# Heads 2 to 30 of an attention kernel: values stationary in the array by quadrants, row sums and normalising on VectorE, the exponent's bound from weight lengths

## The chip, the cores and the metric

The kernel runs on one core of a Trainium2 chip. The metric is the device time of one execution in microseconds (us). A change of less than 0.2% of it is about what a measurement of this kernel cannot tell from none. The engines are named as the profile names them: PE is TensorE's matmuls and PEld its weight loads, DVE is VectorE, ACT is ScalarE, POOL is GpSimd, SP is SyncE, which here only issues DMAs.

## The reference

```
xn = layernorm(x)                                    # x: 2048 x 640, bf16
q  = (xn @ wq)  -> 32 heads of 2048 x 192
s  = softmax(q k^T / sqrt(192)) v                    # k, v: 32 x 2048 x 192
b  = (silu(xn @ w1) * (xn @ w3)) @ w2                # hidden width 1536
out = x + (s @ wo) * silu(b)                         # wo: 6144 x 640
```

## The kernel before

**Tiling.** A head is worked on in four quarters (`qb`) of 512 queries. A quarter has eight steps (`p`), each of which takes 256 keys: two key tiles of 128. Scores come out transposed, keys on the partitions and queries along the row, in a PSUM tile `st2` of 128x1024, of which there are two, used in turn. ScalarE takes the exponent of a whole tile at once into `pT2` (bf16), so no transposition is needed ahead of the values.

**Scores** (`scores`, L472). A head has 192 channels, three times 64. Each matmul contracts 64 channels, so that two of them, one on the upper and one on the lower 64 rows of the array, work at a time. A step has three such pairs, each streaming 512 queries. `qS` and `qD` (made by POOL, L367 and L371) and `KM` (L136, L139) are copies of the queries and keys with their halves swapped, so that every operand stands on the right rows.

**Values** (`values`, L519). The probabilities are the stationary operand, 64 keys by 128 queries, and the values stream: 192 channels and a column of ones, which yields the row sums. That is 193 columns, eight pairs of matmuls a step. The upper and the lower row half accumulate into two parts of each of the two PSUM tiles `ob0` and `ob1`.

**End of a quarter** (`evict`, L493). For each of the two PSUM tiles DVE copies one part (L500), adds the other (L501), takes the reciprocal of the row sums (L506) and scales into the staging tile `ostage` (L507). Every second head, four staging tiles are stored to `o_scr` by DMA (L511).

**The projection of the next head** (`project_chunk`, L340) runs inside the current one: at step 1 of each quarter, `extra` puts ten pairs of 512-column matmuls for one quarter of head h+1 (and, in the spare columns, of the gated layer's hidden units) into a tile of the same two-slot PSUM pool as the scores. DVE casts both halves to `qA` and `qF` (L363, L364).

**The bound of the exponent** (`finish_head`, L447). Softmax is taken without a running maximum. A bound of the scores is subtracted instead: for each channel the largest |k| (six DVE reductions a head, L386) times the largest |q| (two reductions a quarter, L375), summed over channels.

**What sets the order.** Instructions wrapped in `pin` keep the order in which the program issues them on their engine. `advance` (L545) issues scores and the exponent of a step and keeps a list `parts` of pending value matmuls, of which three or four are left when the next step starts; this is why PE always has work while ScalarE computes. Loads of the keys and values of head h+2 are issued on SP at the start of head h (L116, L119), weights on POOL's queue (L105). Head 0 has a hand-written order; heads 1 to 31 run through the loop at L745. After the last head come the rest of the gated layer and the output projection (L820 on), which the diff leaves as they are.

Of the kernel before, what the change touches and what calls it, by code (L numbers as in the profile page):

```python
# [16 lines left out]
P = 128  # L17
# [13 lines left out]
def _kernel_impl(ctx, tc, A_x, A_k_cache, A_v_cache, A_wq, A_wo, B_w1, B_w3, B_w2, out):  # L31
# [124 lines left out]
    with ExitStack() as actx:  # L156
        qp = actx.enter_context(tc.tile_pool(name="qp", bufs=2))
        pp = actx.enter_context(tc.tile_pool(name="pp", bufs=4))
# [150 lines left out]
        def start_head(h):  # L309
            L = loads.pop(h)  # L310
            heads[h] = dict(
                h=h, L=L,
                qA=qp.tile([P, SQ], BF16, tag="qA", name="qA"),
                qF=qfp.tile([P, SQ], BF16, tag="qF", name="qF"),
                qS=qp.tile([P, SQ], BF16, tag="qS", name="qS"),
                qD=qp.tile([DT, SQ], BF16, tag="qD", name="qD"),
                st=stt.tile([P, 5, NQB], F32, tag="st", name="st"),
            )
            pin(nc.vector.memset(heads[h]["st"][:], 0.0))
# [20 lines left out]
        def project_chunk(h, qb, cast=nc.vector.tensor_copy, mid=()):  # L340
# [6 lines left out]
            if h == 0 and qb > 0:  # L347
                by_halves(halves, lambda t, c: wq[:, t, c, :], qs, nc.scalar.copy if qb == 1 else nc.vector.tensor_copy, steps((parts.pop(0),), *mid))
            elif h == 0:
                acc["bp"] = ps_o.tile([P, 2, 512], F32, tag="ob0", name="bp")  # L350
                halves[1] = acc["bp"][:, 1, :]
                for u in (slice(0, 256), slice(256, 512)):
                    for t in range(2):
                        for c in range(DC):
                            pin(nc.tensor.matmul(halves[t][:, u], lhsT=wq[:, t, c, :], rhs=xnT[:, c, u],
                                                 start=(c == 0), stop=(c == DC - 1)))
            else:
                for s in range(2 * DC):
                    for t in range(2):
                        xs = xnT if s % 2 == t else xnS  # L360
                        pin(nc.tensor.matmul(halves[t], lhsT=wq[ROWS[t], s, :], rhs=xs[ROWS[t], s // 2, qs],  # L361
                                             start=(s == 0), stop=(s == 2 * DC - 1)))
            pin(cast(out=qA[:, qs], in_=halves[0]))  # L363
            pin(cast(out=qF[:, qs], in_=halves[1]))  # L364
# [12 lines left out]
            return maxima  # L377
# [6 lines left out]
        def key_maxima(h, j, k=0, n=1):  # L384
            c0, c1 = k * HALF // n, (k + 1) * HALF // n
            pin(nc.vector.tensor_reduce(out=heads[h]["st"][:, j, k:k + 1], in_=heads[h]["L"]["KT"][:, j, c0:c1], axis=AX.X,  # L386
                                        op=ALU.max, apply_absolute_value=True))

# [83 lines left out]
        def scores(hd, qb, p, fill=(0, 0, 0), st2=None):  # L472
# [8 lines left out]
            for s, step in enumerate(steps):  # L481
                keep_busy(fill[s])
                for t, (k, q) in enumerate(step):
                    pin(nc.tensor.matmul(st2[:, t * 512:(t + 1) * 512], lhsT=k, rhs=q[ROWS[t], qs],  # L484
                                         start=(s == 0), stop=(s == 2)))
            return st2

        def weights(st2, nb):
            pT2 = pp.tile([P, 1024], BF16, tag="pT2", name="pT2")
            pin(nc.scalar.activation(out=pT2[:], in_=st2[:], func=ACT.Exp, scale=SCALE, bias=nb[:]))  # L490
            return pT2

        def evict(hd, qb, b, ob):  # L493
            h, hg = hd["h"], hd["h"] % HG
            if b == 0 and hg == 0:
                acc[qb] = stp.tile([P, 4, HG * DH], BF16, tag=f"ostage{qb}", name="ostage")
            ostage = acc[qb]
# [5 lines left out]
            def rest():  # L503
# [3 lines left out]
                pin(nc.vector.tensor_tensor(out=ostage[:, b * 2:b * 2 + 2, hg * DH:(hg + 1) * DH], in0=osum[:, :, 0:DH],  # L507
                                            in1=rl.unsqueeze(2).to_broadcast([P, 2, DH]), op=ALU.mult))
                if b == 1 and hg == HG - 1:
                    g0 = h - hg  # L510
                    acc["store"] = nc.sync.dma_start(  # L511
                        out=o_scr[qb].rearrange("(t p) c -> p t c", p=P)[:, :, g0 * DH:(g0 + HG) * DH], in_=ostage[:, :, :])
# [6 lines left out]
        def values(hd, qb, p, pT2, by_bank=False):  # L519
# [17 lines left out]
            if p == NPAIR - 1 or by_bank:  # L537
                return [lambda b=b: part((0, 1), (b,)) for b in range(2)]
            return [lambda t=t: part((t,), (0, 1)) for t in range(2)]
# [5 lines left out]
        def advance(hd, qb, p, extra=None):  # L545
            pT2 = weights(scores(hd, qb, p), hd["nb"][qb])
            parts.extend(values(hd, qb, p, pT2))
            while len(parts) > (4 if extra else 3):
                parts.pop(0)()
            if extra:  # L550
                extra()
            while late:
                late.pop(0)()

# [47 lines left out]
        def lead():  # L602
            hd, nb = heads[0], heads[0]["nb"][0]
            vals = [values(hd, 0, p, weights(st2, nb), p < 2) for p, st2 in enumerate(early)]
# [4 lines left out]
            vals.append(values(hd, 0, 3, weights(scores(hd, 0, 3), nb)))  # L609
# [3 lines left out]
            vals.append(values(hd, 0, 4, weights(st2, nb)))  # L613
# [9 lines left out]
            parts.extend(vals[4])  # L623
# [4 lines left out]
        def next_part():  # L628
            parts.pop(0)()
# [51 lines left out]
        hTp = fstack.enter_context(tc.tile_pool(name="hTp", bufs=2, side="right"))  # L681
# [8 lines left out]
        def get_hT(qb):  # L690
            if qb not in hTs:
                hTs[qb] = hTp.tile([P, FC - 1, 512], BF16, tag="hT", name="hT")
# [29 lines left out]
        def hidden_last(qb):  # L722
# [3 lines left out]
            for s in range(2 * DC):  # L726
                for t in range(2):
                    xs = xnT if s % 2 == t else xnS
                    pin(nc.tensor.matmul(ps[:, t * 512:(t + 1) * 512], lhsT=w[ROWS[t], s, :], rhs=xs[ROWS[t], s // 2, qs],  # L729
                                         start=(s == 0), stop=(s == 2 * DC - 1)))  # L730
# [14 lines left out]
        for h in range(1, H):  # L745
# [13 lines left out]
            key_slots = list(all_keys)  # L759
            chunks = [[0], [1], [2], [3]] if h + 1 < H else [[0, 1], [2, 3], [], []]  # L760
            gated = []
            for qb in range(NQB):
                post = []

                def extra():
                    if h % 2 == 1:
                        for c in chunks[qb]:
                            gated.append(swiglu_chunk(h // 2, heads[h - 1]["qF"], hd["qF"], c))
                    if h + 1 < H:
                        post.append(project_chunk(h + 1, qb))  # L770
                    else:
                        post.append(hidden_last(qb))

                for p in range(NPAIR):
                    advance(hd, qb, p, extra if p == 1 else None)
# [5 lines left out]
                    if p > 4 and gated:  # L781
                        gated.pop(0)()
                    if h + 1 < H:
                        if p == 2:
                            post.pop()()
                            if qb == NQB - 1:
                                finish_head(h + 1)
                        elif p > 3 and key_slots and (h > 1 or qb > 0):
                            next_keys(h + 1, key_slots)
                    elif p == 3:  # L790
                        gated.append(post.pop()())
            heads.pop(h - 1, None)

# [16 lines left out]
        while len(parts) > 3:  # L810
            parts.pop(0)()
        rest = ffn_hidden(0, 1, ps_st.tile([P, 1024], F32, tag="st2", name="ps_gu"), parts.pop(0))
        load_hT(1)
        while parts:
            parts.pop(0)()
# [331 lines left out]
```

## Time and profile before

| | |
|---|---|
| median of 3 runs | 1937.28 us (1936.53 to 1937.6) |
| the profiled execution: first to last instruction | 1935.5 us |
| granted TensorE clock | 1.000 |
| PE busy | 1927.5 us, 100% of the span |
| ACT busy | 1213.5 us, 63% |
| DVE busy | 1091.5 us, 56% |
| POOL busy | 457.9 us, 24% |
| HBM read and written | 54.26 MB, 31.98 MB |

Rows of the profile's groups name the line, the engine, the operation, what is written and read, the shape and the count, then the busy time, the mean ns of one and the idle time of the engine ahead of them. The timeline lists single instructions with their start and length. A matmul's length in it includes its way through the array, so two rows of the same pair length overlap; the pace is read from the starts.

### The profile page before, as it was taken

How to read it: one execution, taken by the hardware profiler on the slowest of the kernel's cores; microseconds unless marked ns; L12 is line 12 of the kernel's file. 1: busy time of each engine (PE TensorE's matmuls, PEld its weight loads, DVE VectorE, ACT ScalarE, POOL GpSimd, SP SyncE). 2: the span in 40 equal slices, each digit the busy share in tenths (PEclk: the TensorE clock that was granted, in tenths of full speed). 3: DMA queues.
4: the chain of work that ended last, by engine and by line, in shares of the span. 5: the costliest groups of instructions: out<-in, count | busy, mean ns of one | idle time of the engine just before them, and what ended most of it. 6: DMA issues, size and time to landing. Idle time of an engine off the chain costs nothing.

```text
span 1935.5 us, 59521 instructions
## 1 busy us (share of the span) xinstructions
PE 1927.5 (100%) x26720; PEld 1266.1 (65%) x26743; DVE 1091.5 (56%) x2240; ACT 1213.5 (63%) x1173; POOL 457.9 (24%) x757
## 2 busy tenths in 40 slices
PE   9999999999999999999999999999999999999999
PEld 5666666666666666666666677666666666454446
DVE  8665656565656565666655666656665655521111
ACT  7777777777767677777777777777777777210000
POOL 3432222222222222233222222222222220000000
PEclk9999999999999999999999999999999999999999
DMA  7621313121212222242223222213131102946763
GB/s 172 133 71 41 80 41 79 42 71 38 59 41 65 52 55 62 57 95 68 63 50 71 50 71 49 71 41 79 42 79 38 43 10 90 262 93 144 166 151 77
DMA packets 340355, 148.31 MB, mean 77 GB/s; under 512 B 291632, under 2 KB 333584, under 8 KB 340096
## 3 DMA queue, kind: packets, MB, share of 16 engines
q1 hardware_dynamic: 327152, 114.84, 25.7%
q0 software_dynamic: 8256, 24.58, 4.8%
q10 hardware_dynamic: 4688, 5.05, 0.8%
q8 instruction: 210, 3.44, 0.8%
q14 instruction: 49, 0.40, 0.1%
HBM read 54.26 MB, written 31.98 MB: 45 GB/s over the span
## 4 chain that ended last, share of the span: by engine, by line
PE 99%; ACT 0%; issue 0%; DVE 0%; POOL 0%
PE obank L530 35%; PE st L484 34%; PE ps L361 14%; PE ps_s L891 8%; PE ps_s L847 3%; PE ps_f L911 2%; PE ps_gu L704 1%; PE ps_f L927 1%; PE ps L729 0%; PE ps L330 0%; PE fill L207 0%; PE pst L272 0%; PE ps_gu L330 0%; ACT xnT L273 0%; POOL qS L367 0%
## 5 line engine op out<-in xcount | busy, mean ns | idle before, releaser
L490 ACT ACTIVATE pT<-st,nb 128x1024 bf16<-128x1024 f32 x1016 | 1130.8, 1113 | 435.1 <-PE st L484 434.7
L530 PEld LDWEIGHTS <-pT 64*128 64x128 bf16 x16384 | 713.8, 94 | 242.0 <-ACT pT L490 1.5
L530 PE MATMUL obank<-vt,pT 64*128 64x193 bf16 x16384 | 852.3, 243 | 0.2 <-ACT pT L490 0.2
L500 DVE COPY osum<-obank 128x386 f32<-128x386 f32 x256 | 142.4, 556 | 551.4 <-PE obank L530 551.4
L484 PE MATMUL st<-qS,KM 64*128 64x512 bf16 x1023 | 385.2, 377 | 0.5 <-POOL qS L367 0.5
L484 PE MATMUL st<-qD,KT 64*128 64x512 bf16 x1023 | 385.2, 377 | 0.0
L484 PE MATMUL st<-qS,KT 64*128 64x512 bf16 x1023 | 385.1, 376 | 0.1
L484 PE MATMUL st<-qA,KT 64*128 64x512 bf16 x1023 | 385.2, 377 | 0.0
L484 PE MATMUL st<-qA,KM 64*128 64x512 bf16 x1023 | 385.2, 376 | 0.0
L484 PE MATMUL st<-qF,KT 64*128 64x512 bf16 x1023 | 385.1, 376 | 0.0
L367 POOL COPY qS<-qA 64x512 bf16<-64x512 bf16 x256 | 189.4, 740 | 513.8 <-DVE qA L363 482.3
L484 PEld LDWEIGHTS <-KT 64*128 64x128 bf16 x4096 | 202.2, 94 | 135.8 <-issue 0.6
L361 PE MATMUL ps<-xnT,wq 64*128 64x512 bf16 x1240 | 288.1, 376 | 0.0
L361 PE MATMUL ps<-xnS,wq 64*128 64x512 bf16 x1240 | 287.0, 377 | 0.0
L361 PEld LDWEIGHTS <-wq 64*128 64x128 bf16 x2480 | 120.6, 94 | 116.2
L507 DVE TENSOR_TENSOR ostage<-osum,rl_all 128x384 bf16<-128x384 f32 x256 | 153.4, 599 | 8.8
L891 PE MATMUL ps_s<-oT,wo_sb 128*128 128x512 bf16 x705 | 154.9, 379 | 0.8
L501 DVE TENSOR_TENSOR osum<-osum,obank 128x386 f32<-128x386 f32 x256 | 142.6, 557 | 8.9
L891 PEld LDWEIGHTS <-wo_sb 128*128 128x128 bf16 x720 | 70.4, 98 | 85.0 <-issue 0.2
L386 DVE TENSOR_REDUCE st<-KT 128x1 f32<-128x512 bf16 (+1 forms) x189 | 122.0, 685 | 1.2
L484 PEld LDWEIGHTS <-KM 64*128 64x128 bf16 x2048 | 101.0, 94 | 16.5 <-issue 0.5
L105 POOL DMA_DIRECT2D wq<-in_A_wq_dram x62 | 45.7, 737 | 272.8 <-PE ps L361 260.4
(136 smaller groups left out, 1174.6 us busy)
## 6 DMA issues: line engine op xcount, KB each, us to landing
o_scr<-ostage SPq DMA_DIRECT2D x64, 384.0 KB, 2.8
vt<-in_A_v_cache_dram SPq DMA_DIRECT2D x62, 384.0 KB, 4.9
wo_sb<-in_A_wo_dram POOLq DMA_DIRECT2D x1, 7680.0 KB, 32.6
wq<-in_A_wq_dram POOLq DMA_DIRECT2D x31, 160.0 KB, 3.3
hT_scr<-hblk SPq DMA_DIRECT2D x16, 256.0 KB, 3.0
xnS<-xnT POOLq DMA_DIRECT2D x8, 320.0 KB, 7.0
wq<-in_B_w_dram POOLq DMA_DIRECT2D x31, 80.0 KB, 2.6
wq<-in_A_wq_dram POOLq DMA_DIRECT2D x31, 80.0 KB, 2.9
```

The source lines that it names most:

```text
L105: keep(nc.gpsimd.dma_start(out=wq[ROWS[t], :, c0:c1], in_=w.rearrange("(s p) d -> p s d", p=DT)))
L361: pin(nc.tensor.matmul(halves[t], lhsT=wq[ROWS[t], s, :], rhs=xs[ROWS[t], s // 2, qs], start=(s == 0), stop=(s == 2 * DC - 1)))
L367: keep(nc.gpsimd.tensor_copy(out=qS[ROWS[t], qs], in_=qA[ROWS[1 - t], qs]))
L386: pin(nc.vector.tensor_reduce(out=heads[h]["st"][:, j, k:k + 1], in_=heads[h]["L"]["KT"][:, j, c0:c1], axis=AX.X, op=ALU.max, apply_absolu ...
L484: pin(nc.tensor.matmul(st2[:, t * 512:(t + 1) * 512], lhsT=k, rhs=q[ROWS[t], qs], start=(s == 0), stop=(s == 2)))
L490: pin(nc.scalar.activation(out=pT2[:], in_=st2[:], func=ACT.Exp, scale=SCALE, bias=nb[:]))
L500: pin(nc.vector.tensor_copy(out=osum[:], in_=ov[:, 0, :, 0:DH + 1]))
L501: pin(nc.vector.tensor_tensor(out=osum[:], in0=osum[:], in1=ov[:, 1, :, 0:DH + 1], op=ALU.add))
L507: pin(nc.vector.tensor_tensor(out=ostage[:, b * 2:b * 2 + 2, hg * DH:(hg + 1) * DH], in0=osum[:, :, 0:DH], in1=rl.unsqueeze(2).to_broadcas ...
L530: pin(nc.tensor.matmul(acc["o"][b][:, r, (j % 2) * 256:(j % 2) * 256 + DH + 1], lhsT=pT2[ROWS[r], t * 512 + j * P:t * 512 + (j + 1) * P], ...
L847: pin(nc.tensor.matmul(ps, lhsT=oT[:, k, :], rhs=wo_sb[:, k, c0:c1], start=(k == 0), stop=(k == OC - 1)))
L891: pin(nc.tensor.matmul(ps_of[d], lhsT=wo_sb[:, k, d * P:(d + 1) * P], rhs=part(k // KQ)[:, k % KQ, :], start=(k == 0), stop=(k == OC - 1)))
```

## The change

It concerns heads 2 to 30 (`in_quads`).

- **Values** (`values_quads`): the values are now stationary, in blocks of 64 keys by 64 channels, and the probabilities stream. A step streams, for each of the two key tiles, the first 128 channels ("high": four matmuls, one per quadrant of the array, of 512 queries) and the last 64 channels ("low": the two column halves of the array take the two halves of the queries, four matmuls of 256). The output is transposed, channels on the partitions. The column of ones is not used.
- **Scores and projection** in these heads are issued by quadrants too: each matmul with 128 weight columns becomes two with 64.
- **Row sums** (`row_sums`): DVE adds the probability tiles in bf16, two steps' tile at a time: two additions of 2048 a quarter (`fours`), one `join` of 2048, one `fold` of 1024, one of 512 (`ends`). A DMA transpose of the 128x512 result brings the queries onto the partitions; `turned_sums` reduces and inverts it.
- **End of a quarter** (`evict_quads`): ScalarE copies one PSUM tile (128x768), DVE adds the other to bf16, a DMA transpose brings the queries onto the partitions, and two DVE multiplications scale into `ostage`.
- **Bound**: instead of the largest |q|, the length of each weight column times sqrt(640), from a DMA transpose of the weights, two DVE passes of 640 and seven small operations a head (`column_lengths`). The reductions of L375 go, those of L386 become three of 1024 (`fold_keys`).
- **Order**: `step` replaces `advance` from head 1 on; five parts stay pending. DVE's other work is put on a list and issued by `do_chores` after each step within a budget (`ROOM`). The cast of `qF` goes to ScalarE. The probability tiles are three pairs of steps in place of four single steps.

```diff
+    def in_quads(h):
+        return 1 < h < H - 1
...
-        pp = actx.enter_context(tc.tile_pool(name="pp", bufs=4))
+        pp = actx.enter_context(tc.tile_pool(name="pp", bufs=3))
...
+        def by_steps(halves, w, qs, quads):
+            for s in range(2 * DC):
+                for c in ROWS if quads else (slice(0, P),):
+                    for t in range(2):
+                        xs = xnT if s % 2 == t else xnS
+                        pin(nc.tensor.matmul(halves[t][c, :], lhsT=w[ROWS[t], s, c], rhs=xs[ROWS[t], s // 2, qs],
+                                             start=(s == 0), stop=(s == 2 * DC - 1)))
...
-            pin(cast(out=qF[:, qs], in_=halves[1]))
+            pin((cast_low or cast)(out=qF[:, qs], in_=halves[1]))
...
-                for t, (k, q) in enumerate(step):
-                    pin(nc.tensor.matmul(st2[:, t * 512:(t + 1) * 512], lhsT=k, rhs=q[ROWS[t], qs],
-                                         start=(s == 0), stop=(s == 2)))
+                for c in ROWS if quads else (slice(0, P),):
+                    for t, (k, q) in enumerate(step):
+                        pin(nc.tensor.matmul(st2[c, t * 512:(t + 1) * 512], lhsT=k[:, c], rhs=q[ROWS[t], qs],
+                                             start=(s == 0), stop=(s == 2)))
...
+            def sums(t, low):
+                for c in range(2):
+                    c0, q0, n = (P, c * 256, 256) if low else (c * DT, 0, 512)
+                    for r in range(2):
+                        pin(nc.tensor.matmul(acc["o"][r][ROWS[c], int(low), 0:n], lhsT=vt[ROWS[r], t, p, c0:c0 + DT],
+                                             rhs=pT2[ROWS[r], t * 512 + q0:t * 512 + q0 + n],
+                                             start=(p == 0 and t == 0), stop=(p == NPAIR - 1 and t == 1)))
...
+            fs = [lambda: high(0), low, lambda: high(1)]
+            if p in (0, NPAIR - 1):
+                fs = [fs[0], fs[2], fs[1]]
...
+        def evict_quads(hd, qb, banks):
...
+            pin(nc.scalar.copy(out=oa[:], in_=banks[0]))
+            pin(nc.vector.tensor_tensor(out=ot[:], in0=oa[:], in1=banks[1], op=ALU.add))
+            nc.sync.dma_start_transpose(out=ox[:], in_=ot[:])
...
+            if p % 4 == 3:
+                later(1, 1.2, fours)
+            if p == NPAIR - 1:
+                later(1, 1.2, join)
+                later(1, 0.7, fold)
+                later(1, 0.42, ends)
...
+        ROOM = (2.0, 0, 1.25, 1.25, 1.25, 1.25, 1.25, 1.25)
...
+        def do_chores(p):
+            room[0] = min(room[0], 0.6) + ROOM[p]
+            while room[0] > 0.35:
+                ready = [c for c in chores if c[0] <= clock[0]]
...
+        def step(hd, qb, p, extra=None):
...
+            if p == 1 and old_quads:
+                while parts[0][0] != me:
+                    next_part()
+            pT2 = weights(st2, hd["nb"][qb], p)
...
+            if p == 0:
+                while sum(k != me for k, _ in parts) > (2 if old_quads else 1):
+                    next_part()
...
+                while len(parts) > (5 if hd["quads"] else 3):
+                    next_part()
+            if extra:
+                extra()
...
+            clock[0] += 1
+            do_chores(p)
```

More of the change, by code (lines that the diff above doesn't have):

```diff
@@ L608, in lead @@
             vals[0].pop(0)()
-            vals.append(values(hd, 0, 3, weights(scores(hd, 0, 3), nb)))
+            vals.append([f for _, f in values(hd, 0, 3, weights(scores(hd, 0, 3), nb, 3))])
             vals[1].pop(0)()
@@ L725, in hidden_last @@
             ps = ps_st.tile([P, 1024], F32, tag="st2", name="ps")
[L726 to L730, printed above, removed]
+            by_steps((ps[:, 0:512], ps[:, 512:1024]), w, qs, quads)
             pin(nc.vector.tensor_copy(out=g[:, qs], in_=ps[:, 0:512]))
```

264 lines of the change are left out of this document (215 added, 49 removed).

## The prediction

> **What bounds the kernel now.** I read the page first: its busy shares, then the chain that ended last, then the costliest groups.
>
> ```profile
> PE 1927.5 (100%) x26720; PEld 1266.1 (65%) x26743; DVE 1091.5 (56%) x2240; ACT 1213.5 (63%) x1173; POOL 457.9 (24%) x757
> PE 99%; ACT 0%; issue 0%; DVE 0%; POOL 0%
> L490 ACT ACTIVATE pT<-st,nb 128x1024 bf16<-128x1024 f32 x1016 | 1130.8, 1113 | 435.1 <-PE st L484 434.7
> L530 PE MATMUL obank<-vt,pT 64*128 64x193 bf16 x16384 | 852.3, 243 | 0.2 <-ACT pT L490 0.2
> L500 DVE COPY osum<-obank 128x386 f32<-128x386 f32 x256 | 142.4, 556 | 551.4 <-PE obank L530 551.4
> L507 DVE TENSOR_TENSOR ostage<-osum,rl_all 128x384 bf16<-128x384 f32 x256 | 153.4, 599 | 8.8
> L501 DVE TENSOR_TENSOR osum<-osum,obank 128x386 f32<-128x386 f32 x256 | 142.6, 557 | 8.9
> ```
>
> PE is the whole chain, and the others wait for it: ScalarE 435 us for scores, DVE 551 us for output banks. So only two things can move the time: PE's own pace, and a wait that PE does not have today. The pace is in the timeline of one step, and the quarter in a table of stretches (the first stretch begins 0.72 us before a head's first scores; any 12.68 us would do).
>
> ```profile
> 804.03 0.38 PE L484 MATMUL st<-qS,KM 64*128 64x512 bf16 x1
> 804.03 0.38 PE L484 MATMUL st<-qA,KM 64*128 64x512 bf16 x1
> 804.46 0.81 PEld L530 LDWEIGHTS <-pT 64*128 64x128 bf16 x16
> 804.67 0.83 PE L530 MATMUL obank<-vt,pT 64*128 64x193 bf16 x16
> 804.94 1.11 ACT L490 ACTIVATE pT<-st,nb 128x1024 bf16<-128x1024 f32 x1 [0.20 <-PE st L484]
> 805.34 0.38 PE L484 MATMUL st<-qS,KM 64*128 64x512 bf16 x1
> 810.27 0.38 PE L361 MATMUL ps<-xnT,wq 64*128 64x512 bf16 x1
> 812.42 0.38 PE L484 MATMUL st<-qS,KM 64*128 64x512 bf16 x1
> 781.90:794.58 12.68, 12.68 (x200) 8.65 (x196) 10.05 (x18) 9.43 (x10) 4.07 (x6) 1.00 0.55 125
> ```
>
> The two row halves start together (804.03 twice). Three pairs of 512 columns take 804.67 − 804.03 = 0.645 us, 0.215 a pair; the ten of the projection 812.42 − 810.27 = 2.15, the same. Eight pairs of 193 columns take 805.34 − 804.67 = 0.67, 0.083 a pair. Two lengths give 0.00041 us a column and 0.003 a start, so 256 columns take 0.109. PE is busy for all of a quarter's 12.68 us.
>
> **The change part by part, PE.** In a step the values go from 8 × 193 = 1544 columns to 2 × 512 + 2 × 256 = 1536, if four quadrants stream at once. Pace: 2 × 0.215 + 2 × 0.109 = 0.648 against 0.664. Scores and projection keep their columns, with twice the instructions. So a quarter saves 8 × 0.016 = 0.13 us, and 29 heads × 4 quarters = 116 of them save 15 us. More is not there: the array was full before.
>
> No 64x64 matmul is in the trace, so that pace needs bounds. The best: column halves work side by side as row halves do today, 0.648. The worst: they take turns, and a quarter doubles, 12.5 us more (+1450 us). I take the first, since rows of the trace show matmuls on different parts of the array starting within 0.01 us of each other. The issue of instructions is no limit by the next two rows: 24 loads and 24 matmuls ran from 800.40 to 801.40, 21 ns each (the step after begins at 801.40); the changed step has 28 and 28, 56 × 21 = 1.17 us under its 1.29.
>
> ```profile
> 800.18 1.15 PEld L530 LDWEIGHTS <-pT 64*128 64x128 bf16 x24
> 800.40 1.16 PE L530 MATMUL obank<-vt,pT 64*128 64x193 bf16 x24
> 801.40 0.38 PE L484 MATMUL st<-qS,KM 64*128 64x512 bf16 x1
> L530 PEld LDWEIGHTS <-pT 64*128 64x128 bf16 x16384 | 713.8, 94 | 242.0 <-ACT pT L490 1.5
> ```
>
> Weight loads: one of 64x128 takes 94 ns and lies under the matmuls. In the low part each quadrant has 0.109 us per load. If the two quadrants of a row half load in turn at 94 ns, 0.188 is needed and each low set loses 0.08: 2 × 0.08 × 8 × 116 = 148 us. If they load side by side, as row halves do, nothing. I take nothing. [...]
>
> **The end of a quarter.** This is where waits can come from. Durations, from rows:
>
> ```profile
> L466 DVE TENSOR_TENSOR hblk<-pa,qF x16: 416/417/717, 601.8 to 994.6; 64x512 bf16<-64x512 bf16 x16
> L386 DVE TENSOR_REDUCE st<-KT 128x1 f32<-128x512 bf16 x186 | 118.5, 676 | 1.1
> L363 DVE CAST qA<-ps 128x512 bf16<-128x512 f32 x120 | 83.0, 692 | 15.9 <-PE ps L361 0.2
> L464 DVE SCALAR_TENSOR_TENSOR pa<-pt,qF 64x512 bf16<-64x512 bf16 x64 | 46.2, 721 | 0.5
> L506 DVE RECIPROCAL rl_all<-osum 128x2 f32<-128x2 f32 x256 | 41.3, 161 | 4.5
> L707 ACT ACTIVATE t<-ps_gu 128x512 bf16<-128x512 f32 x12 | 7.2, 597 | 20.1 <-PE ps_gu L704 18.0 <-PE ps_gu L330 2.1
> 784.15 0.56 DVE L500 COPY osum<-obank 128x386 f32<-128x386 f32 x1 [5.55 <-PE obank L530]
> 784.74 0.56 DVE L501 TENSOR_TENSOR osum<-osum,obank 128x386 f32<-128x386 f32 x1
> 786.01 0.55 DVE L500 COPY osum<-obank 128x386 f32<-128x386 f32 x1
> 785.54 0.56 DVE L507 TENSOR_TENSOR ostage<-osum,rl_all 128x384 bf16<-128x384 f32 x1
> 26.49 2.14 ACT L490 ACTIVATE pT<-st,nbb 128x1024 bf16<-128x1024 f32 x2
> 27.68 0.51 PE L530 MATMUL obank<-vt,pT 64*128 64x193 bf16 x8 [0.20 <-ACT pT L490]
> ```
>
> The bf16 addition of 512 takes 0.417; L501's 386 f32 columns take 0.557, so a fixed 0.15 and 1.04 ns a column, and half of that a column in the bf16 one. Hence `fours` and `join` (2048) 1.22 each, `fold` (1024) 0.68, `ends` 0.42, the addition of the two banks (768, f32) 0.96, the scalings (512 and 256) 0.69 and 0.42. A reduction of 512 is 0.68, the reciprocal 0.16, the cast 0.69. ScalarE's 768 columns lie between 597 ns for 512 and 1113 for 1024: 0.86. A dependent DVE instruction follows 0.03 after the one before it (784.71 to 784.74), an independent one starts 0.09 early (786.01 against 786.10). Two exponents take 2.14, so the second starts 0.08 early. Scores that stream until 804.67 release ScalarE at 804.94, 0.27 later; ScalarE's first exponent of the pair ended at 27.60 and PE went on at 27.68, 0.08 later.
>
> DVE's sum: before 56% of the span. After, a quarter has 2 × 1.22 + 1.22 + 0.68 + 0.42 + 0.96 + 0.69 + 0.68 + 0.16 + 0.69 + 0.42 = 8.4, and a head adds three reductions of 1024 (3.6), two passes of 640 (1.6, from 0.72 for 512 less its waits), the small ones (some 1.6) and the gate's work (2.3): 42.7, 85% of a head of 50.2. Gone are L375, the second cast and the four L500 to L507 pairs. ScalarE: 8 × 1.113 + 0.86 + 0.6 for the cast + some 0.3 for the gate = 10.7 of 12.5. Neither is full, so it depends on the order. I lay one quarter's end out, 0 being the first scores of the new quarter:
>
> - PE: scores 0 to 0.645; three old parts to 1.29; scores to 1.94; the last two old parts to 2.37; projection to 4.52; scores of step 2 to 5.17, then the new quarter's first values, which overwrite the banks.
> - ScalarE: the last exponent of the old quarter ends at −0.65 + 0.27 + 1.11 = 0.73. Its bank copy is issued ahead of step 1's exponent: 2.37 + 0.27 = 2.64 to 3.50. The exponent then runs 3.42 to 4.53, and PE has it at 4.61, not 4.52: 0.09 late, because scores of step 2 need that slot.
> - DVE: `fours` waits for the last exponent, 0.81; `join`, `fold`, `ends` follow, each on the one before: 0.81 + 1.22 + 1.22 + 0.68 + 0.42 + 3 × 0.03 = 4.44. Only then the banks' addition: 4.35 to 5.31, seen by PE at 5.39. Values were due at 5.17 and with the 0.09 at 5.26: 0.13 more. Behind the addition stands the cast of `qA` (to 5.99); its slot is needed at 6.25, so it holds nobody.
>
> So PE stands 0.22 a quarter; I take 0.2: 116 × 0.2 = 23 us. Bounds: nothing, if the chain of 4.6 us is 5% shorter; 0.2 + 0.45 = 0.65 a quarter, 75 us, if it is 10% longer. Nothing is spare in it, and an addition beside a POOL copy has taken 717 in place of 417 (L466).
>
> **The start of a head.** Here the new DMAs, one transpose of 512 and one of 768 columns a quarter and one of 1280 a head, stand on SP behind the next loads:
>
> ```profile
> 782.19 3.23 SPq L116 DMA_TRANSPOSE KT<-in_A_k_cache_dram  x1
> 785.52 1.14 SPq L119 DMA_DIRECT2D vt<-in_A_v_cache_dram  x2
> 782.62 0.38 PE L484 MATMUL st<-qS,KM 64*128 64x512 bf16 x1
> DMA  3102999799100000000000191000000000047000
> L900 SPq DMA_TRANSPOSE rows<-resT x15: 1210/1222/2356, 1781.7 to 1891.9; - x15
> DMA to landing us min/median/max: 2.4/2.5/4.3
> DMA to landing us min/median/max: 2.6/3.2/7.4
> ```
>
> A 128x512 transpose (L900) lands in 2.5 us, 4.3 at most; of 128x640 at the kernel's start, beside loads, one took 7.4 (last row, line 284). The DMA row has slices of 1 us from 780: the engines are full from 784 to 790, 7.4 after the head's first scores at 782.62. The transpose of the sums is issued at 4.44 and, behind the loads, lands at about 8.7. `turned_sums` has DVE wait for it; behind it stands the next `fours`, 9.5 to 10.7, and for that the exponent of step 6 waits, since there are only three pairs of probability tiles. It is due at 11.0. So 0.3 is spare: nothing. At 7.4 to landing, `fours` would end near 13.9 and PE, which needs that exponent about 0.3 later, would stand 2.6: 29 × 2.6 = 75 us. I take nothing, nearer to L900's like shape. The weight transpose is needed three steps on and squared last of the chores; POOL's copies keep their place; the later hT loads have the last two quarters (25 us) as cover, 5 us if that were gone.
>
> **Sum.** 1935.5 (span) − 15 + 23 = 1943.5. The span is 1.8 under the median of the runs shown, so 1945.
>
> **Rivals.**
> - All is covered (the other side, faster). The mechanism is the order at the quarter's end: bank addition behind the chain from the last exponent. If it reaches PE by 5.17, that is 0.2 earlier than I lay out, only the 15 us of pace are left: 1922. For it: 0.2 in 5.4 us is the size of my error, and one link that is shorter than its row decides. Against: every link is a measured duration, and what I left out lengthens it.
> - No difference: half of the 0.2, 1934 to 1941. The columns are as many as before, so this is near.
> - Weight loads in turn: 1937 − 15 + 148 = 2070 (then the end of the quarter is covered). For it: 94 ns in place of 109 a pair is tight. Against: the array's halves load side by side today.
> - Late transposes or a longer chain: 1945 + 75 = 2020 at the bound, 1970 to 2000 for half.
>
> **How the numbers follow.** Forecast case (slower, 1941 to 1970) 0.39; covered 0.33; within 0.2% 0.15; late transposes or long chain 0.05; weight loads or a slower pace 0.08. Slower is 0.39 + 0.05 + 0.08 = 0.52, faster 0.33, same 0.15; 0.2% (4 us) is about what a measurement of this kernel can tell. The range takes the covered case whole, 1921, and ends at 1995, within the upper bounds; what is beyond has about 0.13. The forecast case alone is 1941 to 1970.
>
> **What would show it.** Pace: starts of 512-column matmuls on one quadrant 0.215 apart, low sets 0.109, steps 1.29 apart. Wait: a PE row "obank <- DVE" (the bank addition) and "st <- ACT" of 0.1 to 0.2, 116 times each, at steps 2 of quarters; DVE near 70% busy over the span. At starts of heads, no ScalarE wait for `fours`. I am wrong if steps are 1.4 or more apart, if PE is as gapless as now, or if PE's waits stand at the start of heads.

## The result, and the profile after

| | before | after |
|---|---|---|
| median of 4 runs | 1937.23 us (1936.53 to 1937.6) | 2065.51 us (2060.33 to 2069.34) |
| ratio, 95% interval | 1 | 1.0661 [1.0645, 1.0677] |
| the profiled execution, first to last instruction | 1935.5 us | 2063.0 us |
| granted TensorE clock | 1.000 | 0.987 |

Slower, as forecast, but by 128 us and not by 8: the time lies outside the range. Names of tiles in the rows: `oa` is ScalarE's copy of one output bank, `ot` the sum of the two banks, `ox` its transpose; `tree` holds the partial row sums, `e` their last sum, `eT` its transpose; `qA` and `qF` are the casts of the two halves of the projection's tile `ps`. From the profile of the changed kernel, its busy shares, the chain that ended last, and the groups of the values' matmuls and of their weight loads:

```profile
PE 1970.8 (96%) x34631; PEld 1316.7 (64%) x34631; DVE 1392.7 (68%) x2326; ACT 1343.1 (65%) x1405; POOL 456.1 (22%) x757
PE 59%; DVE 20%; DMA 12%; ACT 4%; issue 3%; SPq 2%; POOL 0%; DVEq 0%; POOLq 0%
L618 PE MATMUL obank<-pT,vt 64*64 64x256 bf16 (+1 forms) x14848 | 830.4, 327 | 75.4 <-DVE ot L643 72.2
L618 PEld LDWEIGHTS <-vt 64*64 64x64 bf16 x14848 | 516.1, 108 | 251.4 <-issue 106.1
```

PE was the whole chain; now DVE holds 20% of it and DMAs 12%. What replaced "PE waits for nobody" is one line: the values of a new quarter wait for the bank addition (`ot`, L643). The list of waits (who for whom, us in total, times, longest) says what DVE itself waited for:

```profile
ACT qF L371 <- DVE qA L370: 205.4, 116, 5.1
DVE rs L692 <- DMA eT<-e: 93.9, 52, 4.8
PE obank L618 <- DVE ot L643: 72.2, 27, 3.5
DVE ostage L698 <- DMA ox<-ot: 63.1, 22, 3.7
PE st L540 <- ACT qF L371: 9.9, 61, 0.2
```

PE's pace is as predicted. In the timeline the first scores of three steps start 1.30 us apart, and four quadrants start within 0.04:

```profile
809.48 0.38 PE L540 MATMUL st<-qS,KM 64*64 64x512 bf16 x1
809.51 0.38 PE L540 MATMUL st<-qA,KM 64*64 64x512 bf16 x1
809.52 0.38 PE L540 MATMUL st<-qS,KM 64*64 64x512 bf16 x1
809.52 0.38 PE L540 MATMUL st<-qA,KM 64*64 64x512 bf16 x1
810.78 0.38 PE L540 MATMUL st<-qS,KM 64*64 64x512 bf16 x1
812.08 0.38 PE L540 MATMUL st<-qS,KM 64*64 64x512 bf16 x1
```

So the loss is in single places. I measured, in PE's records, the time from the first projection matmul (L348) of one quarter to that of the next, for heads 2 to 30. Before, they are 12.67 or 12.68 us, but for three of up to 12.76. After, by the quarter in which it begins (q0 is a head's first): q0 to q1 13.19, **q1 to q2 16.36**, q2 to q3 12.87, q3 to q0 12.65. Against 12.67 that is 0.52 + 3.69 + 0.20 - 0.02 = 4.39 a head, 29 heads, 127 us, the whole difference. 107 of them are in q1 to q2. The bank addition that ends q0 is issued early in q1, and that is where PE stands. Here is one such q0 in the timeline, with rows of DVE, SP's queue, POOL and ScalarE in order of time; q0's first scores start at 785.03:

```profile
785.95 3.63 SPq L116 DMA_TRANSPOSE KT<-in_A_k_cache_dram  x1
789.37 0.95 DVE L643 TENSOR_TENSOR ot<-oa,obank 128x768 bf16<-128x768 f32 x1
789.68 1.21 SPq L677 DMA_TRANSPOSE eT<-e  x1
790.99 2.24 SPq L119 DMA_DIRECT2D vt<-in_A_v_cache_dram  x2
793.32 2.18 SPq L644 DMA_TRANSPOSE ox<-ot  x1
793.35 1.04 POOL L136 COPY KM<-KT 64x1024 bf16<-64x1024 bf16 x1 [11.78 <-DMA KT<-in_A_k_cache_dram]
793.68 0.69 DVE L692 TENSOR_REDUCE rs<-eT 128x4 f32<-128x512 bf16 x1 [2.76 <-DMA eT<-e]
794.49 2.06 DVE L651 TENSOR_TENSOR tree<-pT,pT 128x2048 bf16<-128x2048 bf16 x1
799.74 0.69 DVE L698 TENSOR_TENSOR ostage<-ox,rl_all 128x512 bf16<-128x512 bf16 x1 [3.18 <-DMA ox<-ot]
802.38 1.23 DVE L651 TENSOR_TENSOR tree<-pT,pT 128x2048 bf16<-128x2048 bf16 x1
805.63 0.42 DVE L651 TENSOR_TENSOR e<-tree 128x512 bf16<-128x512 bf16 x1
805.97 0.95 DVE L643 TENSOR_TENSOR ot<-oa,obank 128x768 bf16<-128x768 f32 x1
807.55 0.59 ACT L371 CAST qF<-ps 128x512 bf16<-128x512 f32 x1 [5.05 <-DVE qA L370]
```

`ot` of the old quarter is ready at 790.3, but its transpose goes out at 793.32, behind the keys and both loads of values, and lands at 799.7. In between DVE has stood 2.76 us for `eT` and 3.18 for `ox`, and one addition took 2.06 in place of 1.23 beside POOL's copies of keys and queries. What DVE did not get done then (squares, `fours`, `join`, `fold`, `ends`) it does ahead of the next bank addition, which ends at 806.9; PE waited 3.34 us there.

The clock is a second loss. The trace has 14 stretches at half clock, 13 of 3.41 us and one of 6.83, each at such a stand of PE; by table of stretches of 1 us (PE, PEld, DVE, ACT, POOL busy, then the granted clock):

```profile
641.00:642.00 1.00, 0.00 (x0) 0.00 (x0) 1.00 (x3) 0.00 (x0) 0.00 (x0) 0.73 0.00 0
643.00:644.00 1.00, 1.00 (x19) 0.71 (x14) 1.00 (x1) 1.00 (x2) 0.94 (x2) 0.50 0.89 167
645.00:646.00 1.00, 1.00 (x28) 0.69 (x23) 0.00 (x0) 0.85 (x1) 0.07 (x1) 1.00 0.18 35
```

PE had stood from 638.5; it goes on at 642.0 with half a clock until 644.9. All stretches together are 51.2 us at 0.5, at most 25.6 us of work.

### The profile page after: what moved, and what is told of

Same layout as the page of the kernel before. It is cut to its first block, busy times and chain, and to the rows that moved or that the text cites. A ratio compares the mean times of both kernels' runs of the same rounds, so it can differ in the third digit from the quotient of the medians.

```text
span 2063.0 us, 75811 instructions
## 1 busy us (share of the span) xinstructions
PE 1970.8 (96%) x34631; PEld 1316.7 (64%) x34631; DVE 1392.7 (68%) x2326; ACT 1343.1 (65%) x1405; POOL 456.1 (22%) x757
## 4 chain that ended last, share of the span: by engine, by line
PE 59%; DVE 20%; DMA 12%; ACT 4%; issue 3%; SPq 2%; POOL 0%; DVEq 0%; POOLq 0%
PE st L540 20%; PE obank L618 16%; DVE tree L651 11%; PE ps_s L1137 8%; DMA ox<-ot 7%; PE ps L348 5%; DMA eT<-e 5%; DVE ot L643 3%; PE obank L598 3%; ACT pT L548 3%; PE ps_s L1093 3%; PE ps_f L1157 2%; SPq L116 2%; DVE qA L370 1%; PE ps_gu L930 1%
## 5 line engine op out<-in xcount | busy, mean ns | idle before, releaser
L618 PE MATMUL obank<-pT,vt 64*64 64x256 bf16 (+1 forms) x14848 | 830.4, 327 | 75.4 <-DVE ot L643 72.2
L618 PEld LDWEIGHTS <-vt 64*64 64x64 bf16 x14848 | 516.1, 108 | 251.4 <-issue 106.1
L540 PE MATMUL st<-qS,KM 64*64 64x512 bf16 (+1 forms) x1951 | 432.7, 381 | 10.2 <-ACT qF L371 9.9
L651 DVE TENSOR_TENSOR tree<-pT,pT 128x2048 bf16<-128x2048 bf16 x232 | 304.6, 1313 | 190.7 <-ACT pT L548 190.2
L540 PE MATMUL st<-qA,KT 64*64 64x512 bf16 (+1 forms) x1951 | 433.0, 380 | 0.0
L540 PE MATMUL st<-qD,KT 64*64 64x512 bf16 (+1 forms) x1951 | 432.6, 380 | 0.0
L540 PE MATMUL st<-qA,KM 64*64 64x512 bf16 (+1 forms) x1951 | 399.9, 383 | 0.0
L540 PE MATMUL st<-qS,KT 64*64 64x512 bf16 (+1 forms) x1951 | 397.4, 380 | 0.1
L540 PE MATMUL st<-qF,KT 64*64 64x512 bf16 (+1 forms) x1951 | 396.7, 380 | 0.0
L540 PEld LDWEIGHTS <-KT 64*64 64x64 bf16 (+1 forms) x7808 | 295.8, 107 | 133.2 <-issue 5.7
L348 PE MATMUL ps<-xnT,wq 64*64 64x512 bf16 (+1 forms) x2390 | 293.2, 376 | 0.0
L348 PE MATMUL ps<-xnS,wq 64*64 64x512 bf16 (+1 forms) x2390 | 288.1, 376 | 0.0
L348 PEld LDWEIGHTS <-wq 64*64 64x64 bf16 (+1 forms) x4780 | 172.1, 106 | 74.2
L692 DVE TENSOR_REDUCE rs<-eT 128x4 f32<-128x512 bf16 x116 | 78.9, 680 | 94.2 <-DMA eT<-e 93.9
L698 DVE TENSOR_TENSOR ostage<-ox,rl_all 128x512 bf16<-128x512 bf16 x116 | 80.4, 693 | 80.4 <-DMA ox<-ot 63.1
```

The lines of the kernel that those rows point to most:

```text
L348: pin(nc.tensor.matmul(halves[t][c, :], lhsT=w[ROWS[t], s, c], rhs=xs[ROWS[t], s // 2, qs], start=(s == 0), stop=(s == 2 * DC - 1)))
L540: pin(nc.tensor.matmul(st2[c, t * 512:(t + 1) * 512], lhsT=k[:, c], rhs=q[ROWS[t], qs], start=(s == 0), stop=(s == 2)))
L618: pin(nc.tensor.matmul(acc["o"][r][ROWS[c], int(low), 0:n], lhsT=vt[ROWS[r], t, p, c0:c0 + DT], rhs=pT2[ROWS[r], t * 512 + q0:t * 512 + q0 ...
L651: pin(nc.vector.tensor_tensor(out=out, in0=a, in1=b, op=ALU.add))
L692: pin(nc.vector.tensor_reduce(out=rs[:], in_=eT[:], axis=AX.X, op=ALU.add))
L698: pin(nc.vector.tensor_tensor(out=stage(h, qb)[:, :, o0:o0 + P], in0=ox[:, 0:4, :], in1=rl.unsqueeze(2).to_broadcast([P, 4, P]), op=ALU.mult))
```

## Experiments

All times stand beside runs of the kernel before, 1936.96 to 1937.17 us on the same chips. The intervals of all kernels, measured as above (mean over heads, us); the sections tell what each kernel is:

| kernel | median | q0 to q1 | q1 to q2 | q2 to q3 | q3 to q0 |
|---|---|---|---|---|---|
| before | 1937.2 | 12.67 | 12.67 | 12.67 | 12.67 |
| after | 2065.5 | 13.19 | 16.36 | 12.87 | 12.65 |
| 1 scale later | 2010.3 | 12.89 | 14.85 | 12.65 | 12.83 |
| 2 loads behind `ox` | 1991.3 | 13.04 | 14.03 | 12.82 | 12.65 |
| 3 no transposes | 1975.6 | 13.02 | 13.51 | 12.82 | 12.64 |
| 4 casts swapped | 2060.6 | 13.28 | 16.09 | 12.81 | 12.65 |
| 5 = 2 and 4 | 1965.2 | 12.67 | 13.61 | 12.81 | 12.65 |
| 6 = 2, fold later | 2049.7 | 12.63 | 16.59 | 12.68 | 12.63 |
| 7 bound's work later | 2022.0 | 13.01 | 14.88 | 12.69 | 13.03 |
| 8 = 6 and 7 | 2054.1 | 12.64 | 16.18 | 12.81 | 13.13 |
| 9 = 5, `KM` by DMA | 1963.3 | 12.66 | 13.61 | 12.74 | 12.69 |
| 10 = 6, loads behind both | 1933.7 | 12.63 | 12.69 | 12.63 | 12.63 |
| 11 = 10, both casts on ACT | 1923.6 | 12.54 | 12.57 | 12.55 | 12.54 |
| 12 = 5, `KM` later | 1948.4 | 12.66 | 12.86 | 12.80 | 12.73 |

Theory at the start: DVE's waits for the transposes that stand behind the loads at a head's start. Rivals: DVE is simply too full; the chain of the old quarter's additions and the casts.

### 1. Let DVE ask for the transposes later

```
-                later(3, 0.9, turned_sums, hd, qb, eT)
+                later(5 if qb == NQB - 1 else 3, 0.9, turned_sums, hd, qb, eT)
```

> The change with one edit: the reduction of the turned sums of a head's last quarter is put on DVE five steps after the sums end, not three. Theory A (at a head's start DVE waits, in order, for transposes that stand behind the next loads on SP, and everything behind it is late): two steps are 2.6 us, most of the 2.8 and 3.2 us that DVE waits there, so the interval from the second to the third projection of a head (16.24 us on average, 12.67 before) falls to about 13.5 and the time by some 80 us, to 1985. Theory B (DVE has too much work in that quarter, whatever it waits for): the work is the same, no more than 10 us, 2055 to 2065.

2010.25 us, ratio 1.0379 [1.0358, 1.0399]: between the two theories. DVE's wait for `eT` fell from 93.9 to 18.3 us, that for `ox` only from 63.1 to 43.3, PE's for `ot` from 72.2 to 40.7. Asking later helps as far as the transpose has landed by then, and `ox` often has not.

### 2. Loads behind the output transpose

The loads of keys and values of head h+2 are issued behind `ox` of the old quarter, and with them POOL's copies of these keys; the rest stays.

```
+            acc["oxd"] = nc.sync.dma_start_transpose(out=ox[:], in_=ot[:])
...
+                    if (qb, p) == (0, 2) and h + 2 < H and h > 1 and in_quads(h - 1):
+                        with tc.issue_after(acc["oxd"].ins):
+                            loads[h + 2].update(load_keys(h + 2))
+                        copy_keys(loads[h + 2], lambda x: x)
```

> The change with one edit: for heads 3 on, the key and value loads of head h+2 are queued on SP behind the output transpose of the head before, where they stood ahead of it. Theory A: the transposes land in 2.5 to 4 us, DVE does not stand, the interval from the second to the third projection returns to 13.0, and of the 128 us lost some 100 come back: 1960. Theory B (DVE full in that quarter): 2065 as before. Theory C (the transposes are slow by themselves, loads or not): 2040 to 2065, and DVE's wait for them stays at 5 us a head.

1991.29 us, ratio 1.0282 [1.0264, 1.0299]; 74 us of the 128 come back with the new order of DMAs on SP. The granted clock is 1.000, against 0.987 in the changed kernel: no stretch at half clock is left inside the heads. The waits of this kernel:

```profile
DVE rs L692 <- DMA eT<-e: 59.4, 54, 2.8
PE obank L618 <- DVE ot L643: 22.4, 22, 1.3
PE st L540 <- ACT qF L371: 11.7, 72, 0.2
DVE ostage L698 <- DMA ox<-ot: 5.4, 8, 0.9
```

That is between the theories: the first asked for 1960, and 30 us remain that this order does not explain, and they sit in q0 to q1 and q1 to q2 again.

### 3. No transposes of sums and outputs

The two DMA transposes are left out and DVE reads their sources, so that the output is not transposed back and the sums are not those of its queries.

```
-            ox = aq["two"].tile([P, 6, P], BF16, tag="ox", name="ox")
-            nc.sync.dma_start_transpose(out=ox[:], in_=ot[:])
+            ox = ot[:].rearrange("p (a b) -> p a b", a=6)
```

> The change without the DMA transposes of the sums and of the outputs: DVE reads the untransposed tiles in their place, so the queries' sums and the output's layout are not turned. Theory A: all of DVE's waits for these DMAs go, intervals of 12.6 to 13.0, about 1950. Theory B: DVE's work is unchanged, 2055 to 2065.

1975.56 us, ratio 1.02 [1.0179, 1.022], between the two theories. So 90 of the 128 us hang on the transposes; 39 do not, although every pace and every column is as predicted. PE still waits for `ot` (9.0 us) and `qF` (11.6).

### 4. ScalarE's cast ahead of DVE's

```
+            if cast_low:
+                pin(cast_low(out=qF[:, qs], in_=halves[1]))
             pin(cast(out=qA[:, qs], in_=halves[0]))
```

> The change with one edit: ScalarE's cast of the projection's second half is issued ahead of DVE's cast of the first. In the profile of the change ScalarE's cast starts 0.04 us after DVE's ends, in all 116 quarters. If that is an ordering that holds PE at the scores of step 3 (0.1 us in good quarters, 0.3 in those of 13.03 us), the good quarters become 12.53 and the time falls by 20 to 25 us, to 2042. If the wait is only reported and PE would have stood anyway for DVE's cast, the time stays within 5 us of 2065.

2060.62 us, ratio 1.0649 [1.0631, 1.0668]: within 5 us of the changed kernel and no gain clear of the noise, as the second expectation had it, while the large waits stand. But the trace answers another question. The wait of ScalarE for DVE is gone, and DVE now waits for ScalarE. Timeline of this kernel, the two casts and PE's next scores:

```profile
605.87 0.59 ACT L371 CAST qF<-ps 128x512 bf16<-128x512 f32 x1 [0.35 <-PE ps L348]
606.48 0.69 DVE L372 CAST qA<-ps 128x512 bf16<-128x512 f32 x1 [0.58 <-ACT qF L371]
607.23 0.37 PE L543 MATMUL st<-qS,KM 64*64 64x512 bf16 x1
```

The two casts, of two halves of one PSUM tile, go one after the other in either order: the traces show the second released by the first, `qF` by `qA` in the changed kernel and `qA` by `qF` here. Together they take 1.28 us, and the scores that need the tile start 0.1 late: 0.96 after the values ahead of them, which began at 606.27 and take 0.87 where nobody waits: 0.65 for 16 (810.13 to 810.78 in the changed kernel) and 0.22 for the other four of 512 columns (809.48 to 809.70).

### 5. Both

> The loads of keys and values behind the output transpose, and ScalarE's cast of qF ahead of VectorE's cast of qA. First theory (the two casts of one tile follow each other, and where the chain of the old quarter's additions stands ahead of VectorE's cast the second cast is late, 0.4 us): quarters of 13.03 us become 12.65 to 12.84, some 10 to 16 us in all, 1975 to 1981. Rival (the order of the two casts is worth nothing, as 2061 against 2066 suggested): within 4 us of 1991.

1965.22 us, ratio 1.0145 [1.0128, 1.0162]: 26 us better than experiment 2, more than expected. With the head's start eased, the order of the casts shows: q0 to q1 comes from 13.04 to 12.67. q1 to q2 comes from 14.03 to 13.61 and no further. The timeline of DVE and POOL at one such q0's end:

```profile
552.73 1.23 DVE L654 TENSOR_TENSOR tree<-pT,pT 128x2048 bf16<-128x2048 bf16 x1 [0.37 <-ACT pT L551]
553.99 2.67 DVE L654 TENSOR_TENSOR tree<-tree 128x2048 bf16<-128x2048 bf16 x2
554.35 1.77 POOL L136 COPY KM<-KT 64x1024 bf16<-64x1024 bf16 x1 [7.70 <-DMA KT<-in_A_k_cache_dram]
556.15 1.40 POOL L139 COPY KM<-KT 64x1024 bf16<-64x1024 bf16 x1
556.69 1.14 DVE L654 TENSOR_TENSOR e<-tree 128x512 bf16<-128x512 bf16 x1
557.75 0.94 DVE L646 TENSOR_TENSOR ot<-oa,obank 128x768 bf16<-128x768 f32 x1
```

`join` and `fold` take 2.67 where they take 1.23 + 0.69 elsewhere (787.04 and 788.29 in the changed kernel's timeline), `ends` 1.14 in place of 0.42. POOL's two copies of the keys run from 554.35 to 557.55, beside them.

### 6. Folding behind the cast

The budget of step 0 is moved to step 2, so that `fold` and `ends` come behind the bank addition and the cast. The loads are as in experiment 2, the casts as in the changed kernel.

```
-        ROOM = (2.0, 0, 1.25, 1.25, 1.25, 1.25, 1.25, 1.25)
+        ROOM = (0.8, 0, 2.45, 1.25, 1.25, 1.25, 1.25, 1.25)
```

> The loads behind the output transpose, and the folding of the sums (fold, ends) behind the bank addition and the cast in every quarter. First theory (fold and ends, 0.7 and 0.4 us, hold the addition and so both casts): quarters 2 to 3, 3 to 0 and 0 to 1 come to 12.54 us, and quarter 1 to 2 loses 0.4 to 0.5, some 25 to 40 us in all: 1951 to 1966. Rival (ScalarE, with copy, exponent and cast in one step, or the two casts alone hold step 3): quarters stay at 12.63 or above, 1975 or more.

2049.71 us, ratio 1.0602 [1.0569, 1.0635]. Three of the four quarters came to 12.63 to 12.68, not to the 12.54 of the first theory: the rival, for which the two casts alone hold step 3, was right there. The fourth went from 14.03 to 16.59, which neither expectation had. `ends` is now later, so the transpose of the sums goes out behind the loads, as the timeline of SP and DVE shows:

```profile
557.28 1.23 SPq L644 DMA_TRANSPOSE ox<-ot  x1
558.62 4.68 SPq L116 DMA_TRANSPOSE KT<-in_A_k_cache_dram  x1
564.01 1.22 SPq L677 DMA_TRANSPOSE eT<-e  x1
568.69 0.69 DVE L692 TENSOR_REDUCE rs<-eT 128x4 f32<-128x512 bf16 x1 [6.42 <-DMA eT<-e]
```

The keys alone held SP for 4.68 us, `eT` went out between the two loads of values and landed 4.7 us after that. DVE stood for it, and the wait that experiment 2 had taken from `ox` came back on the other transpose.

### 7 and 8. The bound's work one quarter later

Squares, roots and reductions of keys for the next head are put on the list in q1 in place of q0 (7: the changed kernel; 8: experiment 6 with it; the budgets of some steps had to be a little larger, 1.4 and 1.6).

```
-                    if p == 3 and (h, qb) != (1, 0):
+                    if p == 3 and qb > 0:
```

> The changed kernel with the squares, roots and key reductions for the next head one quarter later (VectorE has 4 to 7 us less to do in the first quarter of a head); the loads stay where they are. First theory (VectorE stands for the transposes and has no spare time in that quarter to catch up): the wait of PE for the bank addition, 3.3 us a head and some clock with it, goes for the most part, 1965 to 1995. Rival (the transposes alone set when the addition comes): 2050 to 2066.

2021.96 us, ratio 1.0455 [1.0428, 1.0481]: between the two expectations. With less to do in q0, DVE makes up 1.5 of the 3.7 us; the rest it stands for transposes all the same (for `eT` 146.4 us in place of 93.9).

> Loads behind the output transpose, folding behind the cast, squares, roots and key reductions a quarter later. First theory (the three causes found so far are all there is): every quarter comes to 12.54 to 12.67 us, 1922 to 1945, the lower end below the kernel before. Rival (another wait takes their place at the start of a head, such as the later keys or the GpSimd copies): 1955 or more.

2054.14 us, ratio 1.0602 [1.0584, 1.062]: the rival. `eT` still stands behind the loads (DVE waited 163.8 us for it, 6.7 at most). In every other head q3 to q0 takes 13.6 us; the cause of that stays open.

### 9 and 12. POOL's copies of the keys out of the way

Experiment 5 with `KM` made by two DMAs (9), or by POOL's copies queued behind its copy of `qD` of q1 (12).

```
-                        copy_keys(loads[h + 2], lambda x: x)
+                    if (qb, p) == (1, 2) and h + 2 < H and h > 1 and in_quads(h - 1):
+                        with tc.issue_after(acc["qDc"].ins):
+                            copy_keys(loads[h + 2], lambda x: x)
```

> As the run with the loads behind the output transpose and ScalarE's cast first (1965 us), with the second copy of the keys (KM) made by two DMAs in place of two GpSimd copies of 64x1024 a head. First theory (GpSimd's copies, 1.4 to 1.8 us each, run beside join, fold and ends, and stretch those from 2.3 to 3.8 us): quarter 1 to 2 comes from 13.61 to about 12.8, some 20 us, 1943 to 1950. Rival (VectorE's own work or the transposes make that quarter late): 1960 to 1970.

1963.3 us, ratio 1.0124 [1.0107, 1.0141]; the rival's number, but not its reason. PE's wait for `ot` fell from 23.5 to 2.0 us, and in every other head q1 to q2 is 12.67 to 12.84. In the others it goes up to 18.5: DVE's wait for `eT` rose from 50.7 to 84.6 us (4.6 at most), the exponents then waited for DVE (24.4 us), PE for them (16.2). The likely cause is the DMAs that took the copies' place, so I asked again without them; DVE's wait for `eT` is 48.2 us there:

> As the run with the loads behind the output transpose and ScalarE's cast first (1965 us), with GpSimd's two copies of the keys (KM) queued behind its copy of qD of the second quarter, so that they run some 2 us after the bank addition of the quarter's end and not beside join, fold and ends; no DMA is added. First theory (beside these copies join, fold and ends take 3.8 us in place of 2.3, and PE waits for that): quarter 1 to 2 comes from 13.61 to 12.7 to 12.9, 1939 to 1946, and the row of PE waiting for the bank addition, 23.5 us, falls under 5. Rival (the quarter is late for VectorE's own work, or for transposes behind the loads): 1958 to 1970, the row stays near 23.

1948.4 us, ratio 1.0063 [1.0046, 1.008]; 16.8 us better than experiment 5 and 2 above the first theory's range, with the interval and the wait that it asked for. The waits of PE:

```profile
PE obank L622 <- DVE ot L647: 2.4, 12, 0.2
PE obank L622 <- ACT pT L552: 2.0, 3, 1.2
```

The copies beside the chain were most of the wait: 23.5 us became 2.4, and q1 to q2 went from 13.61 to 12.86.

### 10. Loads behind both transposes

Experiment 6, with the loads tied to the transpose of the sums in place of that of the outputs. The keys land later, and so POOL's copies too: in one such stretch they run from 543.39 to 545.71, when `join` is nearly over (542.51 to 543.74) and beside the bank addition (0.95 as ever).

```
-                        with tc.issue_after(acc["oxd"].ins):
+                        with tc.issue_after(acc["eTd"].ins):
```

> As the run with folding behind the cast (2050 us), with the loads of keys and values issued behind both transposes of the old quarter's end, that of the outputs and that of the sums. First theory (that run was slow because the transpose of the sums, now issued later, came to stand behind the loads, and VectorE waits for it up to 7.0 us): quarter 1 to 2 comes from 16.6 to about 12.63 as the others, 2050 - 115 = 1935, up to 1945. Rival (loads of 7 us collide with later transposes wherever they stand, or the order of the additions is what cost): 1980 or more.

1933.66 us, ratio 0.9982 [0.9972, 0.9991]: 116 us less than experiment 6 for the place of three DMAs a head, and 3 us below the kernel before, about the least that can be told from none. The waits that had stood at 139.4 us (DVE for `eT`) and 73.8 (PE for `ot`) in experiment 6:

```profile
DVE rs L692 <- DMA eT<-e: 21.2, 24, 2.5
PE obank L618 <- DVE ot L643: 0.3, 1, 0.3
```

### 11. Both casts on ScalarE

```
-post.append(project_chunk(h + 1, qb, quads=quads, cast_low=nc.scalar.copy if hd["quads"] else None))
+post.append(project_chunk(h + 1, qb, quads=quads, cast=nc.scalar.copy if hd["quads"] else nc.vector.tensor_copy))
```

> As the run before it, with both casts of the projection on ScalarE (0.59 us each) in place of one on VectorE (0.69) and one on ScalarE (0.59), which follow each other. First theory (quarters stand at 12.63 and not 12.54 because the two casts, 1.28 us in turn, end 0.1 us after step 3's scores are due): both take 1.18, quarters 12.54 to 12.55, 1924 to 1935, faster than the kernel before. Rival (ScalarE then has 11.3 us of work in 12.54, its exponents come late, and PE waits for them): slower than the run before it.

1923.59 us, ratio 0.9931 [0.9914, 0.9947]: 10 us less again, faster than the kernel before by 0.7%. The profile of this kernel, busy shares and chain, and PE's waits for DVE in the list of waits:

```profile
PE 1913.8 (100%) x34631; PEld 1516.1 (79%) x34631; DVE 1360.3 (71%) x2210; ACT 1400.5 (73%) x1521; POOL 530.1 (28%) x757
PE 98%; issue 0%; DVE 0%; ACT 0%; POOL 0%; DMA 0%; SPq 0%; POOLq 0%
PE obank L618 <- DVE ot L643: 0.2, 1, 0.2
```

PE is the chain again. The arithmetic of the change is worth 14 us; its order, with the place of one cast, cost 142.

## Why the prediction was wrong

- **Pace: right.** A step 1.30 us (0.648 + 0.645 predicted), a quarter 12.54 where nothing waits (experiment 11): 0.13 under 12.67, as worked out, 15 us.
- **Weight loads and issue: right.** The loads of four quadrants go side by side: in the step that starts at 809.48 four at a time start within 0.04 us of each other. One of 64x64 took 107 to 108 ns by the rows, against 94 for one of 64x128 before, and within the 0.109 us there is. It lies under the matmuls: the steps stay 1.30 us apart (809.48, 810.78, 812.08), for 1.29 predicted.
- **The end of a quarter: right in its place, short in its sum.** In the quarter shown above the bank addition ran from 4.34 to 5.29 us after q0's first scores; I had laid out 4.35 to 5.31. The wait forecast for it came too: of the new quarter's first four matmuls on the values, one starts at 790.22 and three at 790.37, right behind the addition, 0.15 late (0.13 forecast); the list of waits does not count it, since one quadrant was at work. But it is hidden behind a longer wait. The step that failed here is "Behind the addition stands the cast of `qA` (to 5.99) ... it holds nobody". ScalarE's cast of `qF` waits for it, and the two together made step 3's scores 0.1 late at best and 0.5 where `ends` stood ahead (12.63 and 13.03 us a quarter). The three intervals other than q1 to q2 average 12.90, 0.36 above 12.54, against 0.2 taken: 32 us for 87 quarters in place of 17. With 12.90 in q1 to q2 too, the kernel would be 27 us slower than before, within the range; so the direction does not hang on the next step, but the miss of the range does.
- **The start of a head: the step that failed.** "I take nothing, nearer to L900's like shape", bound 75 us. It cost 16.36 - 12.54 = 3.8 us a head, 111 us (some 10 of them the casts of that quarter, by the 0.36 above). The part I had worked out came true: `eT` was there 8.65 us after the head's first scores (8.7 predicted), and the next `fours` started at 9.46 (9.5). But I followed only that transpose. The one of the outputs stands behind two more loads and landed at 14.7 (799.74). DVE waited for it with the squares and four additions queued behind, and all these stand ahead of the next bank addition. I had looked for a wait at the exponent of step 6 and not there. Loads moved behind it: -74 us (experiment 2); behind both: the wait is gone (10).
- **"an addition beside a POOL copy has taken 717 in place of 417 (L466)": seen and not used.** I quoted the row as a doubt on the end of the quarter and gave it no price. Taking the copies away from the chain was worth 17 us (experiment 12 against 5).
- **The rivals.** "Late transposes or a longer chain", 0.05, is what came, and its bound of 2020 was too low, because it counted one transpose, no clock and no second wait. "All is covered, 1922" is what the change gives once its DMAs are in order, folding is moved and both casts are on ScalarE: 1923.6.
- **The clock was in no step.** Stretches at half clock add up to 51.2 us here, at most 25.6 us of work; the bound had no such term.
- DVE near 70% busy: 68%. A share of busy time said nothing on this: it is 71% in experiment 11, where PE's wait for DVE is 0.2 us in all, and within three heads of that kernel 40.2 to 41.0 of 50.2 us (42.7 worked out).

## What to carry to other kernels

When a change puts DMAs on a queue that also issues long loads, write the queue's order down for every one of them, and follow each landing to the next instruction of the engine that waits and on to what is queued behind that; a price for the first of two is no price for both. Move loads with two heads of slack behind transposes with none. An experiment that takes one wait away can bring it back elsewhere (6, 9): read the waits of the new trace before judging the theory by its time.

## What was not expected of the hardware

- **The clock.** Of 24 stands of PE of 2.0 to 3.7 us (from the last matmul's start plus its 0.22), in most heads one, 14 brought half the clock, 13 of them for 3.41 us; one of 2.09 us did, one of 3.50 us (803.47 to 806.97) did not. The 14 stretches at half clock begin on one grid: their starts lie whole multiples of 3.4133 us apart, to 0.01. What goes with the half clock in this trace is how much of one period of this grid PE stood: all 12 stands that cover 2.09 us or more of one were followed by half the clock from that period's end, and 2 of the 12 that cover less. At half the clock, matmuls of 512 columns on one quadrant start 0.43 us apart (643.73 and 644.16) and not 0.215.
- **VectorE beside GpSimd.** An addition with both inputs in SBUF took 2.06 in place of 1.23 us beside POOL's copies (794.49 in the changed kernel), and three of them 3.81 in place of 2.34 (experiment 5). The copies beside the three are longer too (1.40 and 1.77 us in place of 1.04), and so is a copy of the queries beside the one at 794.49 (1.25 in place of 0.61), but not the copy of the keys there (1.04). Not every addition is: the `fold` took 0.68 beside a copy of the queries (experiment 10, 545.90 and 546.05). The bank addition, one input of which is in PSUM, took 0.95 beside a copy (experiment 10, 543.96) and 0.95 without (789.37 in the changed kernel).
- **Landing of a small transpose.** The median from issue to landing is 3.4 us for `eT` and 4.1 for `ox` in the changed kernel. Where the loads stand behind both it is 2.7 and 2.8 in experiment 10 and 3.1 and 2.8 in 11, with the same sizes and the same queue. The longest in the changed kernel are 5.7 and 6.8 us.
